# A planner that sets the issue order: urgency from hand-set positions, or from a backward plan

## The chip, the cores and the metric

The kernel runs on one core of a Trainium2 chip. The metric is the device time of that core in microseconds (us), from the chip's own clock. Five engines matter, and each works through its own instructions in the order in which the program has set them down (for TensorE, VectorE and ScalarE the prediction names the page that says so): TensorE (PE; its weight loads are listed as PEld), VectorE (DVE), ScalarE (ACT), GpSimd (POOL) and SyncE (SP), which issues most transfers. A program on one core has no second core to compare with, so beside every time I look at the mean clock that TensorE was granted in that run (1.000 is full speed).

## The reference

It is the forward pass of a speech joint network and all seven gradients, in bf16:

```python
# x [2,16000,256], w1, w2 [3,256,256], g [2,8,256], w_f, w_g, w_o [256,256]
h = gelu(conv3(x, w1))[:, ::2]                       # [2, 8000, 256]
f = gelu(conv3(h, w2))[:, ::2]                       # [2, 4000, 256]
fe, ge = f @ w_f, g @ w_g
j   = tanh(fe[:, :, None, :] + ge[:, None, :, :])    # [2, 4000, 8, 256]
out = j @ w_o
# returns out and the gradients of x, w1, w2, g, w_f, w_g, w_o for a given grad_out [2,4000,8,256]
```

The joint has 8 label positions for each of the 8000 time steps, so `out`, `grad_out` and the products with `w_o` are where most of the bytes and matmuls are.

## The kernel before

The kernel cuts time into 18 chunks over two batches (most of them 512 output steps wide) and does each chunk in stages: A (convolutions, `FE`, and `FER`, which is `FE` transposed), J (joint, `out` and its gradient) and DE (backward to `x`). No stage issues an instruction directly. It *records* operations, with the engines that may run them, a duration by the program's own model, and what they read and write. When everything is recorded, a list scheduler, here called the planner, sets the operations down one by one. The order on each engine, and for many copies the engine itself, come out of this planner (shortened, with comments added; cuts are marked):

```python
class Flow:
    WAKE = {"PE": 45.0, "ACT": 25.0, "DVE": 25.0, "POOL": 280.0, "SP": 60.0}
    MARGIN = 6500.0
    TAIL = {"PE": 180.0, "ACT": 130.0, "DVE": 95.0, "POOL": 40.0, "SP": 0.0}
    # ...
    def op(self, eng, cost, fn, r=(), w=(), new=(), at=None, ..., margin=None):
        o.margin = self.MARGIN if margin is None else margin
        o.prio = (self.now if at is None else at, o.n)      # the hand-set position
        # ... dependences and buffers
    def issue(self):
        # ...
        while left:
            best = None
            for e, lst in avail.items():                    # every engine
                t, cand = T[e], None                        # T: when it is free in the plan
                for o in lst:                               # every operation that is ready
                    s = o.ready + wake                      # ... and its buffers are free
                    k = (max(s, t), o.prio, o, e)
                    if cand is None or k < cand:
                        cand = k
                if cand is not None and (best is None or cand[0] < best[0]):
                    best = cand
            s, _, o, e = best
            T[e] = s + o.cost[o.eng.index(e)]
            if o.work:                                      # a transfer
                # ...
                o.done = ring[e] + 2000.0 + o.margin
            else:
                o.done = T[e] + self.TAIL[e]
            o.inst = o.fn(e)                                # the instruction is emitted here
            # ...
```

Among operations of one engine that could start equally early, the one with the smallest `prio` wins, a position set by hand. And a transfer, unless it is given a margin of its own, is assumed to land 2000 + 6500 ns after its turn on its ring: `MARGIN` is an allowance, so that the plan does not rest on a transfer that comes late.

The copies out of PSUM may go to either of two engines, whichever the planner can start first.

```python
    def evac(dst, src, n, r, w, new=(), scale=None, eng=("ACT", "DVE"), f=1.0):
        # ... a copy by ScalarE or by VectorE
        return op(eng, ..., go, r=r, w=w, new=new)

    # stage A, once per chunk, for mt in 0, 1
    pe_first(mt == 0, "fe", c_pe([W] * KT), mms, r=[(FT, 0), (FT, 1), WF], w=[ps], ...)
    evac(lambda mt=mt: FE[:, mt, :W], lambda ps=ps: ps[:, :W], W, r=[ps], w=[(FE, mt)])
    S["FER"] = to_rows("fer", FE, 0, nb_of[g_] * P, [0, 1, "z"])   # PE transposes FE: 8 matmuls
```

## Time and profile before

| | before |
|---|---|
| time, 3 runs | 800.54 us (800.07 to 802.18) |
| profiled span | 798.8 us |
| TensorE busy / matmul stream worked out | 773.6 us / 762.0 us |
| not stream | 36.8 us |
| VectorE busy, ScalarE busy | 748.7 us, 713.7 us |

"Stream" is what the matmuls alone would take with none ever waiting; the prediction below tells how it is counted. The difference, "not stream", is all that an order can win back, and much of it is fixed (the first input must arrive, the last output must leave). A useful tool is the running sum: at a matmul that both programs have, take its start time and subtract the stream of all matmuls before it. What is left is the time lost up to there. In the trace of before that sum is 20.5 us at 159 us, 23.6 at 429, 25.55 at 567, 28.3 at 765 and 36.8 at the end.

The second is the view of transfers in the last 29 us before the end (what was moved, queue, kind, number, and the median us from issue to landing):

```profile
GHeR<-GHe SPq DMA_TRANSPOSE x2, 3.6
...
HRs<-HTo SPq DMA_TRANSPOSE x2, 2.8
...
NFR<-NGFE SPq DMA_TRANSPOSE x1, 2.4
```

With little other traffic the transposes land 2.4 to 3.6 us after their issue. The planner reckons with 8.5 us plus the transfer itself.

### The profile page before, as it was taken

Reading aid. Unit: us, or ns where it says so; the run is one execution under the profiler, and the core shown is the slowest. Engines: PE = TensorE matmul, PEld = TensorE weight load, DVE = VectorE, ACT = ScalarE, POOL = GpSimd, SP = SyncE. Lnnn points to the kernel's source line nnn. Section 1 sums busy time; section 2 is a strip of 40 time slices with the busy share of each in tenths; the row PEclk is TensorE's granted clock in tenths of the full one; section 3 lists DMA queues with packets and bytes.
Section 4 is the critical chain, followed back from the end, with each engine's and each line's share of the span. In section 5 each row is a group of like instructions: output and inputs, shape, how many; then the busy total and the mean of one; then the engine's idle time right before and its main releaser. Section 6 shows DMA issues by size and latency. Waiting matters only on the chain.

```text
span 798.8 us, 17636 instructions
## 1 busy us (share of the span) xinstructions
PE 773.6 (97%) x6196; PEld 576.0 (72%) x6196; DVE 748.7 (94%) x1752; ACT 713.7 (89%) x1177; POOL 209.1 (26%) x452
## 2 busy tenths in 40 slices
PE   7799999999999999999999999999999999999996
PEld 5566667686776867787877677676776867778885
DVE  4999999998989999998999999998989999999986
ACT  6999999999898989988789999999898989988861
POOL 1212322122222222333232231332222222223242
PEclk9999999999999999999999999999999999999999
DMA  8999999999999999999999999999999998998994
GB/s 205 218 218 226 248 243 228 248 249 273 242 255 245 220 255 192 256 223 256 215 220 209 231 245 240 252 268 257 248 234 246 232 251 208 254 228 206 204 200 104
DMA packets 384701, 184.75 MB, mean 231 GB/s; under 512 B 331716, under 2 KB 368358, under 8 KB 384612
## 3 DMA queue, kind: packets, MB, share of 16 engines
q1 hardware_dynamic: 366644, 133.25, 86.2%
q0 software_dynamic: 15584, 49.19, 18.8%
q10 hardware_dynamic: 2384, 1.18, 0.6%
q8 instruction: 48, 0.79, 0.4%
q14 instruction: 41, 0.34, 0.2%
HBM read 52.48 MB, written 50.34 MB: 129 GB/s over the span
## 4 chain that ended last, share of the span: by engine, by line
PE 66%; DVE 16%; ACT 10%; issue 4%; DMA 2%; POOL 1%; SPq 1%; POOLq 0%; ACTq 0%; DVEq 0%
PE ps L343 56%; PE GWO L343 10%; DVE NGZ L764 3%; DVE ZS L772 2%; DVE g_s L530 2%; ACT JT L697 2%; ACT g_s L536 2%; ACT g_sq L526 1%; ACT OUT_SB L354 1%; ACT FE L354 1%; DMA GOT<-GO_R 1%; DMA XC<-in_x_dram 1%; DVE g_sq L543 1%; PE psb L583 1%; DVE g_sq L541 1%
## 5 line engine op out<-in xcount | busy, mean ns | idle before, releaser
L697 ACT ACTIVATE JT<-FE,GE 128x512 bf16<-128x512 bf16 (+2 forms) x288 | 187.9, 684 | 0.5 <-DVE FE L359 0.2
L371 POOL DMA_DIRECT2D out_dram<-OUT_SB x136 | 94.9, 698 | 347.1 <-ACT OUT_SB L354 285.8
L343 PE MATMUL ps<-GOT,WT 128*128 128x512 bf16 (+3 forms) x640 | 151.9, 332 | 2.1 <-DMA GOT<-GO_R 2.1
L764 DVE SCALAR_TENSOR_TENSOR NGZ<-JSQ,ps 128x512 f32<-128x512 bf16 (+2 forms) x252 | 151.8, 607 | 0.6 <-PE ps L343 0.6
L343 PE MATMUL ps<-WO,JT 128*128 128x256 bf16 x1024 | 151.5, 272 | 0.3 <-DVE g_s L530 0.3
L354 ACT CAST OUT_SB<-ps 128x512 bf16<-128x512 f32 x223 | 132.7, 600 | 15.8 <-PE ps L343 15.7
L717 ACT ACTIVATE JR<-JR 128x1024 bf16<-128x1024 bf16 x128 | 138.1, 1082 | 5.7 <-DVE JR L710 5.4
L343 PE MATMUL GWO<-GO_R,JR 128*128 128x256 bf16 x1024 | 132.7, 273 | 4.3 <-ACT JR L717 4.3
L343 PEld LDWEIGHTS <-JT 128*128 128x128 bf16 x1024 | 98.9, 98 | 46.0 <-issue 1.4
L772 DVE TENSOR_TENSOR ZS<-ZS,NGZ 128x512 f32<-128x512 f32 (+2 forms) x216 | 131.7, 614 | 0.2
L754 ACT ACTIVATE JSQ<-JT 128x1024 bf16<-128x1024 bf16 (+2 forms) x121 | 116.2, 960 | 13.6 <-DVE NGZ L764 12.6
L343 PEld LDWEIGHTS <-JR 128*128 128x128 bf16 x1028 | 99.8, 98 | 26.8 <-ACT JR L717 6.1
L343 PEld LDWEIGHTS <-WT 128*128 128x128 bf16 x1000 | 87.7, 98 | 38.6 <-DMA GOT<-GO_R 2.4
L343 PEld LDWEIGHTS <-W 128*128 128x128 bf16 x792 | 69.7, 98 | 54.4 <-issue 2.8
L343 PE MATMUL ps<-XC,W 128*128 128x512 bf16 (+4 forms) x432 | 92.6, 342 | 2.3 <-DMA XC<-in_x_dram 1.5
L710 DVE TENSOR_TENSOR JR<-FER,GEB 128x1024 bf16<-128x1024 bf16 x128 | 87.5, 685 | 0.4 <-PE GWO L343 0.4
L343 PEld LDWEIGHTS <-X 128*128 128x128 bf16 x768 | 75.0, 98 | 9.6
L530 DVE SCALAR_TENSOR_TENSOR g_s<-g_sq,ps 128x512 bf16<-128x512 bf16 (+2 forms) x108 | 65.9, 612 | 13.4 <-ACT HTo L528 9.2
L343 PE MATMUL ps<-WT,GHo 128*128 128x256 bf16 x384 | 73.3, 273 | 0.5 <-DVE NGZ L764 0.3
L825 DVE TENSOR_TENSOR ACC<-ACC,ps 128x512 f32<-128x512 f32 x96 | 63.8, 679 | 6.0 <-PE ps L343 5.8
L526 ACT ACTIVATE g_sq<-ps 128x512 bf16<-128x512 f32 (+2 forms) x108 | 60.0, 555 | 8.9 <-PE ps L343 8.0
L371 POOL DMA_DIRECT2D out_dram<-GX_SB x70 | 39.1, 559 | 104.3 <-ACT GX_SB L356 49.6
(139 smaller groups left out, 1269.3 us busy)
## 6 DMA issues: line engine op xcount, KB each, us to landing
GO_R<-in_grad_out_dram SPq DMA_DIRECT2D x120, 256.0 KB, 3.9
out_dram<-OUT_SB POOLq DMA_DIRECT2D x120, 256.0 KB, 4.5
X<-in_x_dram SPq DMA_DIRECT2D x28, 576.0 KB, 5.6
out_dram<-GX_SB POOLq DMA_DIRECT2D x60, 256.0 KB, 4.1
GOT<-GO_R SPq DMA_TRANSPOSE x128, 5.3
out_dram<-w_out SPq DMA_DIRECT2D x9, 128.0 KB, 2.0
GO_R<-in_grad_out_dram SPq DMA_DIRECT2D x8, 128.0 KB, 3.2
out_dram<-OUT_SB POOLq DMA_DIRECT2D x8, 128.0 KB, 4.4
```

The costliest lines, as they stand in the source:

```text
L343: nc.tensor.matmul(ps_ap, lhsT=lhsT, rhs=rhs, start=start, stop=stop)
L354: nc.scalar.copy(out=dst(), in_=src())
L371: return eng_.dma_start(out=out(), in_=in_())
L526: op("ACT", c_act(W, True), lambda e, mt=mt, ps=ps: nc.scalar.activation(out=sq[:, mt, :W], in_=ps[:, :W], func=ACT.Square, scale=GELU_SQR ...
L530: op("DVE", c_dve(W), lambda e, mt=mt, ps=ps: nc.vector.scalar_tensor_tensor(out=s[:, mt, :W], in0=sq[:, mt, :W], scalar=1.0, in1=ps[:, :W ...
L697: op("ACT", c_act(W, ptr=True), lambda e, j=j, mt=mt: nc.scalar.activation(out=JT[:, j, mt, :W], in_=S["FE"][:, mt, :W], func=ACT.Tanh, bi ...
L710: op("DVE", c_dve(n * 2 * D, 0.5), lambda e, lo=lo, n=n, m=m, JR=JR: nc.vector.tensor_tensor(out=JR[:m, lo % 2:lo % 2 + n], in0=S["FER"][: ...
L717: op("ACT", c_act(n * 2 * D), lambda e, lo=lo, n=n, m=m, JR=JR: nc.scalar.activation(out=JR[:m, lo % 2:lo % 2 + n], in_=JR[:m, lo % 2:lo % ...
L754: nc.scalar.activation(out=JSQ[:, :, :W], in_=JT[:, j, :, :W], func=ACT.Square)
L764: op("DVE", c_dve(W) + 6, lambda e, d2=d2, ps=ps, u=u, zap=zap, JSQ=JSQ: nc.vector.scalar_tensor_tensor(out=zap(), in0=JSQ[:, d2, :W], sca ...
L772: op("DVE", c_dve(W), lambda e, d2=d2, dst=dst, NGZ=NGZ: nc.vector.tensor_tensor(out=dst[:, d2, :W], in0=ZS[:, d2, :W], in1=NGZ[:, :W], op ...
L825: op("DVE", c_dve(512), lambda e: nc.vector.tensor_tensor(out=acc_ap().rearrange("p k d -> p (k d)"), in0=acc_ap().rearrange("p k d -> p ( ...
```

## The change

The intent: replace the hand-set position by an urgency that follows from the work itself. The planner first runs forward as before. Then it goes backward from the planned end: each operation must be done before the latest start of all that need it, minus the signalling time, and must share its engine with the others that are as late; what comes out is its latest start. That is the new key among operations that could start equally early. Forward and backward are repeated, and the plan is emitted whose TensorE ends first by the planner's own durations. The work is the same: 6196 matmuls before and after. The core of the diff (cut; the rest is bookkeeping so that a plan can be made without being emitted):

```diff
-        o.prio = (self.now if at is None else at, o.n)
+        o.pos = self.now if at is None else at
+        o.key = (o.pos, o.n)
@@
-    def issue(self):
+    def issue(self, passes=3):
+        best = None
+        for k in range(passes + 1):
+            end = self.run(False)
+            if best is None or end < best[0]:
+                best = (end, [o.key for o in self.ops])
+            if k < passes:
+                self.backward(end)
+        for o, key in zip(self.ops, best[1]):
+            o.key = key
+        self.run(True)
+
+    def backward(self, end):
+        # ... succ: for each operation, what needs it, and after what lag
+        for o in sorted(self.ops, key=lambda o: -o.seqn):
+            e, c = o.at[0], o.at[2] - o.at[1]
+            E = end
+            for d, lag in succ[o]:
+                x = late[d] if lag < 0 else late[d] - self.WAKE[d.at[0]] - lag
+                E = min(E, x)
+            # ... move E earlier past what already occupies engine e
+            late[o] = E - c
+        for o in self.ops:
+            o.key = (late[o], o.n)
@@
-                    k = (max(s, t), o.prio, o, e)
+                    k = (max(s, t), o.key, o, e)
```

More of the change, by code (lines that the diff above doesn't have):

```diff
@@ L40 @@
 class Op:
-    __slots__ = ("eng", "cost", "fn", "deps", "succ", "left", "prio", "new", "bufs", "done", "work", "n", "ready", "inst", "hold", "nb", "lead", "margin")
+    __slots__ = ("eng", "cost", "fn", "deps", "succ", "left", "prio", "new", "bufs", "done", "work", "n", "ready", "inst", "hold", "nb", "lead", "margin", "pos", "key", "at", "slotdeps", "seqn")
 class Flow:
@@ L53, in __init__ @@
         self.ctx, self.tc, self.ops, self.slots, self.now, self.seq = ctx, tc, [], {}, 0.0, {}
+        self.bufs = []
     def cls(self, name, n, any_order=False, psum=False):
@@ L57, in cls @@
             name=f"{name}{i}", bufs=1, **({"space": bass.MemoryType.PSUM} if psum else {}))) for i in range(n)]
-        self.slots[name] = [[p, 0.0, None] for p in pools]
+        self.slots[name] = [[p, 0.0, []] for p in pools]
         self.seq[name] = [0, 0, any_order]
@@ L97, in op @@
                 bufs.append(b)
+            self.bufs.append(b)
         o.bufs = bufs
@@ L105, in op, with run @@
         return o
-    def issue(self):
+    def issue(self, passes=3):
[10 more added lines that the diff above has]
+    def backward(self, end):
+        late, busy = {}, {e: [] for e in self.WAKE}
+        succ = {o: [] for o in self.ops}
+        for o in self.ops:
+            for d in o.deps:
+                succ[d].append((o, d.done - d.at[2]))
+            for d in o.slotdeps:
+                succ[d].append((o, self.TAIL[d.at[0]]))
+            for b in o.bufs:
+                if b.born is not None and b.born is not o:
+                    succ[b.born].append((o, -1e9))
+        for o in sorted(self.ops, key=lambda o: -o.seqn):
[4 more added lines that the diff above has]
+                E = min(E, x)
+            iv = busy[e]
+            i = len(iv)
+            while i:
+                lo, hi = iv[i - 1]
+                if hi <= E - c:
+                    break
+                if lo < E:
+                    E = lo
+                i -= 1
+            iv.insert(i, (E - c, E))
+            late[o] = E - c
+        for o in self.ops:
+            o.key = (late[o], o.n)
+    def run(self, emit):
         T = {e: 0.0 for e in self.WAKE}
@@ L112, in issue @@
         left, prog = len(self.ops), -1e12
-        slots, seq = self.slots, self.seq
+        slots = {k: [[p, 0.0, []] for p, _, _ in v] for k, v in self.slots.items()}
+        seq = {k: [v[0], 0, v[2]] for k, v in self.seq.items()}
+        users, use = {}, {}
+        for o in self.ops:
+            o.left = 0
+            for b in o.bufs:
+                users[b] = users.get(b, 0) + 1
+        for o in self.ops:
+            for d in o.succ:
+                d.left += 1
+        num = 0
         def put(o):
@@ L157, in issue @@
             if o.lead:
-                prog = max(prog, o.prio[0])
+                prog = max(prog, o.pos)
             for x in o.eng:
                 avail[x].remove(o)
+            o.slotdeps = []
             for b in o.new:
@@ L164, in issue @@
                 b.slot, slots[b.cls][i][1] = i, None
+                if not seq[b.cls][2]:
+                    o.slotdeps += slots[b.cls][i][2]
+                slots[b.cls][i][2] = []
                 seq[b.cls][1] += 1
-                b.t = slots[b.cls][i][0].tile(b.shape, b.dtype, name=b.name, tag=b.cls)
+                if emit:
+                    b.t = slots[b.cls][i][0].tile(b.shape, b.dtype, name=b.name, tag=b.cls)
             T[e] = s + o.cost[o.eng.index(e)]
@@ L180, in issue @@
                 o.done = T[e] + self.TAIL[e]
-            o.inst = o.fn(e)
-            for h in o.hold:
-                self.tc.add_manual_dep(o.inst.ins, h.inst.ins.name, mybir.DependencyInfo(
-                    mybir.DependencyClass.Sync, mybir.DependencyReason.DATA), reason="order of the first loads")
+            o.at, o.seqn = (e, s, T[e]), num
+            num += 1
+            if emit:
+                o.inst = o.fn(e)
+                for h in o.hold:
+                    self.tc.add_manual_dep(o.inst.ins, h.inst.ins.name, mybir.DependencyInfo(
+                        mybir.DependencyClass.Sync, mybir.DependencyReason.DATA), reason="order of the first loads")
             left -= 1
             for b in o.bufs:
-                b.users -= 1
-                if b.users == 0 and b.cls is not None:
+                if b.cls is not None:
+                    slots[b.cls][b.slot][2].append(o)
+                users[b] -= 1
+                if users[b] == 0 and b.cls is not None:
                     slots[b.cls][b.slot][1] = o.done
@@ L193, in issue @@
                     put(d)
-        self.T = T
+        return T["PE"] if not emit else T
 def c_pe(ns):
```

## The prediction

> **What bounds the kernel now.** I read the profile from coarse to fine: busy times, busy shares in slices, stretches of 20 us, TensorE's waits, and then the timelines of the first 30 us and the last 24 us. The first lines say which engine is fullest and whether that holds all along.
>
> ```profile
> PE 773.6 (97%) x6196; PEld 576.0 (72%) x6196; DVE 748.7 (94%) x1752; ACT 713.7 (89%) x1177; POOL 209.1 (26%) x452
> ...
> PE   7799999999999999999999999999999999999996
> ...
> DVE  4999999998989999998999999998989999999986
> ACT  6999999999898989988789999999898989988861
> ```
>
> TensorE (PE) is busy 97%, but VectorE (DVE, 94%) and ScalarE (ACT, 89%) are close, so I ask stretch by stretch which one is full. The rows below are from the table of 20 us stretches: PE, PEld, DVE, ACT and POOL busy time, then clock, DMA share, GB/s.
>
> ```profile
> 20.00:40.00 20.00, 15.19 (x118) 10.67 (x117) 19.17 (x56) 19.82 (x38) 4.13 (x9) 1.00 1.16 218
> 40.00:60.00 20.00, 18.28 (x136) 12.29 (x136) 19.57 (x53) 19.79 (x33) 3.30 (x7) 1.00 1.04 217
> ...
> 320.00:340.00 20.00, 20.00 (x173) 15.45 (x171) 19.24 (x45) 18.85 (x35) 5.53 (x14) 1.00 1.13 257
> ...
> 780.00:800.00 20.00, 12.38 (x117) 9.83 (x114) 11.18 (x35) 3.36 (x6) 4.76 (x12) 0.92 0.40 102
> ```
>
> Three regimes: from 20 to about 120 us DVE and ACT are both full and PE has holes; from 120 to 760 us PE is full; at the end a chain of dependences runs with every engine partly idle.
>
> A busy PE is not a streaming PE, so I add up the stream itself. Counting matmuls by width (4308 of 256 columns, 1064 of 512, 468 of 128, 168 of 384, 160 of 160 or 32, few others) at columns/2.4 + 2.5 ns, with 25 ns as the least, gives **762.0 us**. The trace supports the rate: in the last run of 256-column weight-gradient matmuls, 22 of them go from 791.60 to 794.01 us, 109.5 ns each against 109.2. So of the 798.8 us span, **36.8 us** is not stream. Doing the same sum per stretch puts 17.2 us of it before 80 us (7.0, 5.4, 2.3, 2.5), 2.2 us at 80 to 120, 7.7 us from 780 us to the end, and the remaining 9.7 us thinly over the 660 us between. TensorE's waits name the holes (total us, times, longest):
>
> ```profile
> PE GWO L343 <- ACT JR L717: 4.3, 5, 1.8
> PE psb L583 <- ACT FE L354: 3.4, 9, 0.5
> PE ps L343 <- DMA GOT<-GO_R: 2.1, 1, 2.1
> PE ps L343 <- DMA XC<-in_x_dram: 1.5, 1, 1.5
> PE ps L343 <- DVE NGFE L772: 1.4, 1, 1.4
> PE ps L343 <- DVE gT L1080: 1.3, 1, 1.3
> ...
> PE psb L583 <- DVE FE L359: 0.7, 2, 0.5
> ```
>
> The second and last rows are the one repeating hole of the middle: once per chunk the transposes of FE come too soon after FE was copied out, 0.3 to 0.5 us, **4.1 us** in all. The others happen at the start or the end.
>
> **What the Trainium skill says.** "TensorE: Matmul & The Clock Gate", section "Back-to-back issue gap", gives columns/2.4 + 2.5 ns for an isolated gap; the trace agrees (above). The same section has about 131 ns for 512 columns in sustained LDWEIGHTS-MATMUL pairs; the trace does not agree: six such matmuls from 18.76 to 20.05 us are 215 ns each, and I use that. "Perfetto Trace Analysis", section "Per-engine timelines", says that ACT and DVE are strict FIFO and that TensorE only pulls weight loads ahead. That is why the program's order matters here: an operation set down too early stalls everything behind it on its engine, as the FE holes show. The same page, section "Optimization Strategy", says a kernel can have several regimes and may gain by interleaving them; the three regimes above are such a case, and a planner's order is what could interleave them.
>
> **The change part by part.** No operation's work is changed: the same 6196 matmuls, the same buffers, the same transfers. Before, the planner ran once, and among operations that could start equally early took the one with the smallest hand-set position. Now it runs forward, then computes backward from the end how late each operation may start, uses that as urgency, repeats three times, and emits the plan whose TensorE ends first by its own durations. Comparing the two programs' orders per engine shows what moved:
>
> 1. *FE gets more lead.* I counted how many ns of matmul stream stand in the program between the copy of FE and its transposes. With ACT as the copier, 39 of 81 uses had under 1000 ns before, 15 of 97 now; the 5% point goes from 551 to 820 ns. The copy takes 584 ns (ACT) plus signalling, so most of the 4.1 us of holes should close: estimate **-3.0 us**. FT (16 uses under 1000 ns, now 6) and GF (12, now 4) move likewise: their waits are small, with the batch switch near 430 us (hole 1.1 us) I put **-1.0 us**.
> 2. *The choice of engine shifts.* 15 OUT_SB copies, 7 net FE copies of several widths and 3 GX copies go from ACT to DVE, 11 squares (JSQ) from DVE to ACT, 4 FER copies from DVE to ACT; shifts of G1S go to POOL, of GFS to DVE. With durations of the trace: DVE +10.2 (15 x 0.683) +4.6 (FE) +2.0 (GX) -7.5 (11 x 0.684) -2.5 (FER) and about -1.3 for the small ones, **+5.5 us** on DVE; ACT **-0.8 us** (-9.0 -4.0 -1.8 +11.9 +3.6 -1.5). In the middle this is free: DVE has 50 us of idle time. In the first 120 us it isn't. When the stream has reached 80 us, the new order has set down about 5 us more of DVE and ACT work together than the old one; those two engines have only 3.4 us of idle time between 20 and 100 us, so about 1.6 us over two engines is real delay: estimate **+1.0 us**.
> 3. *The very start.* The loads of WF and WO now come before W2, and the GEB matmuls before the second convolution. This moves the second convolution later by perhaps 1 to 2 us. But the first product with GOT waits for its transfer in the old trace:
>
> ```profile
> 26.89 1.05 PE L343 MATMUL ps<-GOT,WT 128*128 128x256 bf16 x8 [2.10 <-DMA GOT<-GO_R]
> ```
>
> The work set before that product is the same in both orders, and so are the transfers ahead of it. The 2.1 us absorb the delay: **0**.
>
> 4. *The end.* The old order ran all 24 weight-gradient matmuls of the previous block and then stood 1.43 us at NGFE (row above). The new one puts 8 of them between each pair of NGFE and GF products, which fills that hole: **-1.4 us**. In exchange, the X rows of the last block can be loaded only after those matmuls have freed their buffer, and the load now stands in SP's queue behind the transpose GHeR. In the old trace that transpose was issued at 788.69 us and PE came for X at 791.6, 2.9 us later; now X needs 1.26 (issue of GHeR) + 0.6 (its own) + about 2 (landing, from the 2.0 us of w_out) = 3.9 us: **+1.0 us**. The 4.6 us after the last matmul stay.
>
> Sum: -3.0 -1.0 +1.0 +0 -0.4 = **-3.4 us**; 800.5 - 3.4 = 797.1, which I round to **797.2 us**.
>
> **The rivals.** *A: the start gets clearly shorter.* 17.2 us are lost before 80 us; if the backward plan postpones work that isn't urgent, PE could gain 5 to 8 us there, giving 790 to 793 us. For it: that is where a backward plan should help most. Against it: by 80 us of stream the new order has done more DVE and ACT work, not less. *B: the real machine punishes the plan.* Waits on single DMA arrivals appear because latest-time urgency drops slack that the hand-set positions had; at 10 waits of 1 us, 808 us. For it: the DMA share is over 1 in most stretches, and X's least lead at the end falls from 6.2 to 3.1 us of stream. Against it: the median lead of GOT (21.3 to 22.2 us) and GO_R (39.4 to 39.6 us) is unchanged, since buffers and not urgency decide when they start. *C: nothing moves,* 800 us: the FE holes close but DVE, fuller by 5.5 us, opens others.
>
> **Range and chances.** A gain over 2% needs 16 us out of 36.8, of which 7.3 (first input's arrival) and 4.6 (after the last matmul) are out of reach: 0.03. A loss over 2% needs 16 us of new stalls: 0.02. Between A and B the range is 791.5 to 803.5 us.
>
> **What would show it.** Right: the FE waits of TensorE fall from 4.1 to about 1 us; the NGFE wait vanishes and a wait on X of about 1 us appears near the end; the GOT wait near 27 us shrinks; PE's busy time stays at 20 of 20 us in the middle. Wrong: if PE in 20 to 120 us is fuller by 4 us or more, rival A; if new DMA waits turn up in the middle, rival B; if PE's wait for FE stays, step 1 was mis-sized.

## More of the kernel before

Besides the lines that the prediction shows, two views of the trace before are needed later. The first is the pair of 20 us stretches around the point where the second batch begins to flow in (columns: the stretch, its length, busy time of PE, PEld, DVE, ACT, POOL, then clock, DMA share, GB/s):

```profile
420.00:440.00 20.00, 19.36 (x153) 14.04 (x151) 19.72 (x50) 19.62 (x32) 5.11 (x11) 1.00 1.18 211
440.00:460.00 20.00, 20.00 (x141) 13.27 (x139) 19.86 (x44) 20.00 (x32) 5.29 (x13) 1.00 1.10 238
```

VectorE and ScalarE are full here, as they are in the first 120 us, though TensorE is full too.

## The result, and the profile after

The changed kernel took **802.34 us** (median of 6 runs, 800.52 to 803.2) beside 801.36 us for the kernel before in the same rounds (6 runs, 800.07 to 802.63). The ratio is 1.0009, with a 95% interval of 0.9993 to 1.0026: no difference that the runs can tell. (Ratios here are the mean time of one kernel's fast runs over the mean of the other's fast runs of the same rounds, so not quite the ratio of the medians quoted. All runs in this document were correct.) Both kernels' times mostly follow the granted clock: the changed one had 800.52 us at 0.999 and 803.2 at 0.995, the one before 805.97 at 0.99 in a later round (one run of it, 803.79 at 1.000, doesn't fit). At equal clock the two agree: at 0.997 the changed kernel took 801.93 and 802.74, the one before 801.19 to 802.74 over all rounds. That scatter of a few us is as large as what is sought, so the traces must show where the time went.

The head of the page of after, whose columns are those of the prediction's first fence:

```profile
span 800.2 us, 17623 instructions
...
PE 775.6 (97%) x6196; PEld 576.2 (72%) x6196; DVE 754.2 (94%) x1756; ACT 715.2 (89%) x1164; POOL 223.2 (28%) x461
...
DVE  5999999998989999997989999999999999999995
```

VectorE is busy 5.5 us longer, just what counting the moved copies had said. TensorE does the same matmuls in 2 us more. The span is 1.4 us longer than before.

TensorE's waits in the trace of after (what waited, for what, us in all, times, longest):

```profile
PE GWO L412 <- ACT JR L786: 3.3, 3, 1.5
PE psb L652 <- DVE FE L428: 3.2, 4, 1.6
PE ps L412 <- DVE NGZ L833: 2.3, 3, 0.9
...
PE psb L652 <- ACT FE L423: 0.9, 3, 0.5
...
PE ps L412 <- DMA GOT<-GO_R: 0.4, 1, 0.4
```

The waits that the change was to close add up to as much as before, under another name. Waits for FE were 3.4 us on ScalarE and 0.7 on VectorE, 4.1 together; now they are 0.9 on ScalarE and 3.2 on VectorE, 4.1 together again. ScalarE's nine short holes have become three; VectorE's two have become four, and these are longer. Here is one of the four in the timeline of after from 38 to 45 us (start, busy us, engine, line, what, how many; in brackets the idle time before it and what ended that):

```profile
40.75 0.59 ACT L423 CAST FE<-ps 128x512 bf16<-128x512 f32 x1
...
42.92 0.68 DVE L428 CAST FE<-ps 128x512 bf16<-128x512 f32 x1
...
43.66 0.56 PE L652 MATMUL psb<-ident,FE 128*128 128x128 bf16 x7 [1.58 <-DVE FE L428]
```

The first half of FE was copied by ScalarE from 40.75 us, the second by VectorE, which got to it only at 42.92 us, 2.2 us later. The transposes need both. The matmuls that the second copy waits for had ended by 41.58 us, and the trace shows VectorE without a gap from there to the copy: the lead that the plan gave was spent in VectorE's line. This half was VectorE's in the kernel before, too, with a hole of 0.50 us. And the longer hole took the place of others: the running sums of the two traces are only 0.2 us apart at 50 us (14.1 before, 14.3 after).

The stretches of after answer to those shown of before:

```profile
20.00:40.00 20.00, 15.86 (x123) 10.88 (x121) 19.49 (x55) 20.00 (x39) 5.16 (x10) 1.00 1.16 242
40.00:60.00 20.00, 17.23 (x130) 11.71 (x129) 19.64 (x55) 19.61 (x33) 3.24 (x8) 1.00 0.96 206
...
420.00:440.00 20.00, 19.25 (x155) 13.95 (x154) 20.00 (x46) 19.02 (x30) 5.85 (x11) 1.00 1.16 237
440.00:460.00 20.00, 19.22 (x139) 13.08 (x138) 20.00 (x44) 19.91 (x30) 3.89 (x6) 1.00 1.11 252
...
780.00:800.00 20.00, 14.77 (x139) 11.41 (x136) 11.50 (x31) 4.71 (x10) 5.74 (x14) 0.98 0.44 115
```

In 40 to 60 us TensorE has 1.05 us less than before. Around the batch switch VectorE has no idle time at all, 20.00 of 20 in both stretches, and TensorE falls from 20.00 to 19.22 us in the second. In the last stretch TensorE does more (139 matmul instructions where before had 117), in part only because this span ends 1.4 us later; the running sum below is the fairer measure of the end.

At the very end, the wait for NGFE that the prediction named is gone, and the one product that waits noticeably waits for something else. From the timeline of after:

```profile
782.82 0.30 PE L412 MATMUL ps<-NGFE,WT 128*128 128x160 bf16 x2
...
791.05 0.37 PE L412 MATMUL ps<-JR 8*128 8x256 bf16 x2 [0.93 <-ACT JR L423]
...
793.12 0.41 PE L412 MATMUL ps<-GHoR,X 128*128 128x256 bf16 x2
```

The first and last line carry no bracket: neither NGFE nor X was waited for.

The running sum of time lost puts these together. The figures are what each part adds to it, from one trace of each kernel; the right pair is a cleaner one (experiments 3 and 4), in which both profiles had a clock of 0.999 and the same span of 800.3 us, with the marker in parentheses where it differs. (Its sum is 36.8 because its 14 added warm-up matmuls put 1.5 us more into the stream.)

| part | before | after | difference | clean pair: before, after, difference |
|---|---|---|---|---|
| start, to 160 us | 20.5 | 22.2 | +1.7 | 20.3, 21.0, +0.7 |
| 160 to 430 us (520) | 3.1 | 2.5 | -0.6 | 4.2, 5.9, +1.7 |
| 430 (520) to 570 us | 1.95 | 5.0 | +3.05 | 0.5, 1.5, +1.0 |
| 570 to 765 us (733) | 2.7 | 1.4 | -1.3 | 2.2, 1.3, -0.9 |
| from there to the end | 8.5 | 7.1 | -1.4 | 9.6, 7.1, -2.5 |
| sum | 36.8 | 38.2 | +1.4 | 36.8, 36.8, 0.0 |

So the change does move time. It gains 2.7 us (3.4 in the clean pair) after 570 us, and loses 4.15 us (3.4) before.

### The profile page after: what moved, and what is told of

Read it like the earlier page. It is cut to its first block, busy times and chain, and to the rows that moved or that the text cites. A ratio compares the mean times of both kernels' runs of the same rounds, so it can differ in the third digit from the quotient of the medians.

```text
span 800.2 us, 17623 instructions
## 1 busy us (share of the span) xinstructions
PE 775.6 (97%) x6196; PEld 576.2 (72%) x6196; DVE 754.2 (94%) x1756; ACT 715.2 (89%) x1164; POOL 223.2 (28%) x461
## 4 chain that ended last, share of the span: by engine, by line
PE 68%; DVE 19%; ACT 10%; issue 2%; DMA 1%; DVEq 0%; ACTq 0%
PE ps L412 58%; PE GWO L412 9%; DVE NGZ L833 4%; DVE ZS L841 3%; ACT JT L766 2%; DVE g_s L599 2%; DVE JR L779 2%; ACT JR L786 2%; DVE ACC L894 1%; ACT g_sq L595 1%; ACT JSQ L823 1%; DVE g_sq L610 1%; ACT g_s L605 1%; DVE GHo L954 1%; DMA XC<-in_x_dram 1%
## 5 line engine op out<-in xcount | busy, mean ns | idle before, releaser
L766 ACT ACTIVATE JT<-FE,GE 128x512 bf16<-128x512 bf16 (+2 forms) x288 | 182.0, 676 | 5.8 <-PE ps L412 5.6
L786 ACT ACTIVATE JR<-JR 128x1024 bf16<-128x1024 bf16 x128 | 136.4, 1070 | 6.6 <-DVE JR L779 6.5
L823 ACT ACTIVATE JSQ<-JT 128x1024 bf16<-128x1024 bf16 (+2 forms) x132 | 126.6, 960 | 7.7 <-DVE NGZ L833 5.7
L423 ACT CAST OUT_SB<-ps 128x512 bf16<-128x512 f32 x208 | 119.2, 598 | 8.4 <-PE ps L412 8.2
```

Source lines behind the costliest of these rows:

```text
L423: nc.scalar.copy(out=dst(), in_=src())
L766: op("ACT", c_act(W, ptr=True), lambda e, j=j, mt=mt: nc.scalar.activation(out=JT[:, j, mt, :W], in_=S["FE"][:, mt, :W], func=ACT.Tanh, bi ...
L786: op("ACT", c_act(n * 2 * D), lambda e, lo=lo, n=n, m=m, JR=JR: nc.scalar.activation(out=JR[:m, lo % 2:lo % 2 + n], in_=JR[:m, lo % 2:lo % ...
L823: nc.scalar.activation(out=JSQ[:, :, :W], in_=JT[:, j, :, :W], func=ACT.Square)
```

## The experiments

Fourteen kernels ran. Each time is compared with the kernel before in the same rounds on the same chip. In experiments 1, 2, 5, 6 and 9 to 12 the planner's first pass, which is the plan by hand-set positions, is barred from being emitted; the diffs below leave that line out. The expectations call theories by letters.

### 1 and 2: the end alone, and the body alone

Does the change gain at the end and lose in the body? Then keeping the old plan up to 745 planned us (experiment 1) should beat both kernels, and keeping it after that (experiment 2) should lose. The rival: the two are not separable, or nothing is going on and both are as before. `s0` holds the planned starts of the first pass, which is the plan of before.

```diff
             self.backward(end)
+            for o, t in zip(self.ops, s0):
+                if t < 745e3:          # experiment 2: if t >= 745e3
+                    o.key = (t, o.n)
```

> Old order (planned start of the first forward pass as key) for everything the plan starts before 745 us, backward urgency for the rest. Theory T (the backward plan pays with TensorE holes at the start and at the batch switch, 20.8 us of non-stream before 120 us against 19.4 and 29.7 at 550 us against 25.5, for a shorter end): this order keeps the small holes and gets the better end, so 0.5 to 1.5 us under the kernel before (ratio about 0.9985), cumulative non-stream at the last chunk's NGFE product about 30 us, not 31.5. Rival C (the difference is only the clock at the start): within 0.3 us of before. The planner's own estimate is 2.6 us better than before.

> The reverse: backward urgency before 745 us planned, old order after it. Theory T: the payment without the gain, 2 to 3 us over before (ratio about 1.003), with the batch-switch holes (430 to 550 us) of about 3 to 5 us as in the changed kernel. Rival C: same as before within 0.3 us. Rival D (all differences are noise of the plan, not located): anything between 0 and 2 us with holes elsewhere.

Experiment 1: 801.6 us beside 801.62, ratio 0.9993 (0.9973 to 1.0014). Experiment 2: 807.1 us, ratio **1.0065** (1.0044 to 1.0085). The body under the new urgency, with the old end, is clearly slower; its running sum is 22.95 us by 161 us, 30.1 at 572 and 34.2 at the last NGFE product (before: 20.5, 25.55 and 30.5). Part of this is clock: its runs had 0.992 to 0.994. But at 0.994 it took 806.7 to 808.1 us, where before, in other rounds, took 802.7 to 803.9. Experiment 1 has roughly the body of before, and did not get the end of the changed kernel: TensorE still waits 1.0 us for NGFE, and 0.5 us for X, and from 765 us on its trace loses 8.4 us, where before loses 8.5 and the changed kernel 7.1. So the loss in the body is shown by time; the gain at the end, so far, by the traces of the changed kernel alone.

### 3 and 4: is it the clock at the start?

In the trace of after the first 12 us ran partly at a lower clock. This is where each kernel's first convolution starts, after the run of warm-up matmuls, in the timeline of TensorE; first before:

```profile
7.27 1.25 PE L343 MATMUL ps<-XC,W 128*128 128x256 bf16 x10 [1.45 <-DMA XC<-in_x_dram]
```

and after:

```profile
7.21 2.29 PE L412 MATMUL ps<-XC,W 128*128 128x256 bf16 x10 [2.06 <-DMA XC<-in_x_dram]
```

The same ten matmuls took 2.29 us in place of 1.25, following a hole of 2.06 us in place of 1.45; the granted clock from 6 to 12 us was 0.79, 0.50 and 0.86 in stretches of 2 us. A rival explanation of the whole result is therefore that the start's clock hides a gain. A longer warm-up should close that hole in both kernels, and then after should be ahead:

```diff
-        for _ in range(20):
+        for _ in range(34):
@@
-    op("PE", 20 * 215.0, warm_up, r=[(warm, 0)], w=[wps], new=[wps])
+    op("PE", 34 * 215.0, warm_up, r=[(warm, 0)], w=[wps], new=[wps])
```

> Kernel before with 34 instead of 20 warm-up matmuls, so that TensorE does not pause before the first convolution at 7.2 us. Rival C (a half clock in the first convolution: 2.29 us for ten matmuls in the changed kernel's trace, 1.25 in before's): mean clock 0.999 or more in all runs, spread of the times smaller, time lower by up to 1 us on average. Theory T says nothing against that, but expects the same gap between the two orders with warm clocks.

> Changed kernel with 34 warm-up matmuls. Rival C: equal to e3 within 0.3 us, the whole loss of the change being the cold clock. Theory T: about 1 us slower than e3, with the cumulative non-stream at 550 us some 3 us over that of e3.

Before with the long warm-up took 803.78 us, ratio 1.0026 (1.0003 to 1.0049); after with it 802.69 us, ratio 1.0015 (0.9994 to 1.0037). The longer warm-up starts the first convolution 0.34 us later than before (7.61 us), at full clock in both profiles, but does not cure the scatter of clocks over the runs (0.992 to 0.999 in experiment 3). What counts is the comparison of the two profiles, both at 0.999: the same span, 800.3 us. With equal clocks the change still brings nothing, so this rival fell. The trace of after says the same: by 40 us its running sum is 12.5 us, that of before 12.7, so the slow start had already been taken up by shorter waits. The pair is the clean one of the table above.

### 5 and 6: whose order does it, TensorE's or the others'?

Every operation's key was changed at once. Experiment 5 gives the backward urgency to TensorE's operations alone, experiment 6 to all but TensorE's:

```diff
             self.backward(end)
+            for o, t in zip(self.ops, s0):      # s0: the hand-set keys
+                if o.eng != ("PE",):            # experiment 6: ==
+                    o.key = t
```

> Backward urgency as key for TensorE's operations alone; all other engines keep the old positions. Theory T2 (the harm is the new order on VectorE and ScalarE, the good is TensorE's order at the end): holes up to 560 us as in the kernel before (25 to 26 us of non-stream, not 29.7), end as good as in the changed kernel (24 weight-gradient matmuls around NGFE); 1 to 2.5 us under before, ratio about 0.998. Rival P (TensorE's own new order delays the next chunk's VectorE and ScalarE work at the batch switch): 1 to 3 us over before, the batch-switch holes still 4 us.

> The reverse: backward urgency for VectorE, ScalarE, the transfers and POOL, old positions on TensorE. Theory T2: 2 to 4 us over before (ratio about 1.004), with the end of the kernel before. Rival P: at most 1 us over before, the batch-switch holes as in the kernel before (2 us between 430 and 550 us).

Experiment 5: 799.48 us beside 801.95, ratio **0.9968** (0.9951 to 0.9985). Experiment 6: 806.42 us, ratio **1.006** (1.004 to 1.008). They part on either side of 1, and both intervals are clear of it. The gain of experiment 5 lies at the end: its running sum is 20.8 us by 160 us and 28.1 at 762 (before: 20.5 and 28.3), then 28.6 at the last NGFE product with 8.7 us of stream left, where before has 30.5 with the same 8.7 left. Half of that is given back after it, 1.03 us in one wait on VectorE for `ngb`: the sums end at 35.8 and 36.8. Its FE holes are those of before, 4.2 us in all (a row of its waits):

```profile
PE psb L654 <- ACT FE L425: 3.1, 8, 0.5
...
PE psb L654 <- DVE FE L430: 1.1, 2, 0.6
```

So TensorE's new order is worth some 2 us (at a clock of 0.997, 799.4 to 800.2 us beside 801.95; at 1.000, 798.64 and 798.88 beside 800.59 and 800.64, with a third run of before at 803.79), and did not need the FE holes for it. Experiment 6 loses from the start on: 24.9 us by 163 us, 32.0 at 571, 36.4 at the last NGFE product. Its profiled run is the one with the lowest clock, 0.990; but at 0.996 and 0.997 it took 804.9 to 806.1 us, before 801.95 to 802.72, so the loss is there at equal clock. Its timeline shows one way in which a late engine costs more than its lateness:

```profile
28.16 1.86 PE L414 MATMUL ps<-GOT,WT 128*128 128x256 bf16 x8 [3.07 <-DMA GOT<-GO_R]
```

Before has the same product after a hole of 2.10 us, and then its eight matmuls took 1.05 us. Here the hole is 3.07 us and they took 1.86 us, because the clock had been lowered, as the stretch shows in the column after the five engines:

```profile
28.00:30.00 2.00, 1.84 (x9) 1.28 (x9) 1.22 (x6) 1.32 (x2) 0.00 (x0) 0.50 1.20 326
...
34.00:36.00 2.00, 2.00 (x21) 1.79 (x19) 1.83 (x8) 1.11 (x3) 0.69 (x1) 1.00 1.21 296
```

There are 9 matmul instructions in the first of these stretches against 21 at 34 us; in the trace's record of the clock the half speed lasts from 26.7 to 33.5 us. In this run the hole is paid twice. It is not its length alone that decides this: in experiment 10 a hole of 1.42 us had slow matmuls after it as well, 1.72 us for the same eight:

```profile
26.46 1.72 PE L414 MATMUL ps<-GOT,WT 128*128 128x256 bf16 x8 [1.42 <-DMA GOT<-GO_R]
```

### 7: closing the FE holes directly

If the FE holes cost their 4.1 us, then telling the planner of before that a copy of FE lands 700 ns later than its model says should close them and win about 3 to 4 us. The rival: the planner will push something else into the way.

```diff
-                o.done = T[e] + self.TAIL[e]
+                o.done = T[e] + self.TAIL[e] + o.lag          # o.lag: 0.0 unless set
@@
-            evac(lambda mt=mt: FE[:, mt, :W], lambda ps=ps: ps[:, :W], W, r=[ps], w=[(FE, mt)])
+            evac(lambda mt=mt: FE[:, mt, :W], lambda ps=ps: ps[:, :W], W, r=[ps], w=[(FE, mt)]).lag = 700.0
```

> Kernel before, but the planner is told that a copy of FE takes effect 700 ns later, so that the transposes of FE stand later in TensorE's order. It measures my step 1 by itself. If the holes are an order fault, TensorE's waits for FE fall from 4.1 us to under 1 and the time falls 2.5 to 3.5 us (ratio 0.996 to 0.997). Rival F: the holes only move to other waits because VectorE or ScalarE is the limit there: waits for FE fall, time within 1 us of before.

Measured: 801.15 us beside 801.95, ratio 0.9992 (0.9976 to 1.0008). The rival was right in the total, and the theory in the middle. From the waits:

```profile
PE ps L344 <- DMA GHeR<-GHe: 2.5, 1, 2.5
...
PE psb L584 <- ACT FE L355: 0.5, 1, 0.5
```

The FE waits fell to about 0.6 us, and between 162 and 347 us the running sum stood still at 23.3, where that of before grew from 20.8 (at 161 us) to 23.1: the holes of the middle are real losses. But the start came out 2.8 us worse, with a new wait of 2.5 us for a transfer at 129.6 us, and the batch switch about 2 us worse. The likely reason, which was not tested by itself, is that a 700 ns request moves everything after it, in the stretches where VectorE and ScalarE have no room.

### 8: an honest margin at the end

Why does the planner choose a plan that is worse in the body? Its own reckoning (numbers of the planner, not times) puts the end of TensorE at 789.49, 789.36, 788.24 and 790.26 us for the four plans, so it emits the third and *itself* expects to gain 1.25 us. In that plan the time lost before the end is 4 us more than with hand positions (16.7 against 12.7 us at 736 us of stream), and the last 27 us of stream lose 8.2 in place of 13.4 us. It pays 4 us to save 5 in an end that it takes to be long, since it allows each transpose its 6.5 us of margin there. On the chip those transposes land in 2.4 to 3.6 us in all. If this is right, a margin of 500 ns for the transposes of the last two chunks should make it keep the hand positions:

```diff
-            bytes_=KT * n * P * P * 2, new=[R], transpose=True, nb=nb, at=at)
+            bytes_=KT * n * P * P * 2, new=[R], transpose=True, nb=nb, at=at,
+            margin=500.0 if g_ >= NG - 2 else None)
```

> Changed kernel, but the planner counts the row transposes of the last two chunks with 0.5 us of margin instead of 6.5 us; nothing else. The planner itself then keeps its first forward pass, as none of the backward plans ends earlier. Theory T (the 6.5 us margin made a long imaginary end, for whose shortening the backward plan paid elsewhere): start and middle holes of the kernel before, time 0 to 1 us under before. Rival M (the margin is right, landing late matters): new TensorE waits on the row transposes at the end, 1 us or more over before.

With it the planner's four ends are 780.23, 783.52, 784.38 and 784.19, and it emits the first, the plan by hand-set positions. It took 799.79 us beside 801.95, ratio **0.9971** (0.9955 to 0.9988). The running sum is that of before (20.1 at 159 us, 25.6 at 567, 28.2 at 765) up to the end, where the wait for NGFE shrinks from 1.4 to 0.2 us. The time gained is more than the 0 to 1 us expected, but in part that is scatter: at a clock of 1.000 it took 799.25 to 799.82 us and before 800.59 and 800.64 (a third run 803.79), and the two traces differ by 1.0 us (35.8 and 36.8). So the NGFE hole, the only gain of the changed kernel that I had got right, came from too large an allowance for these transfers and can be had by one argument, with no backward plan at all. That the planner's trade was driven by the margin is shown by its choice; that the margin is also why the body of the chosen plan loses on the chip is not.

### 9, 10, 13 and 14: is it the choice of engine?

In the body, both the order on VectorE and ScalarE changed, and which of the two makes a copy. The theory: the choice of engine is the culprit, as the FE holes suggest. Three of these kernels freeze each copy on the engine that it has in the plan of before (9, 10 and 14), and one (13) leaves the choice free:

```diff
             end = self.run(False)
+            if k == 0:
+                for o in self.ops:
+                    if len(o.eng) > 1:
+                        o.cost = (o.cost[o.eng.index(o.at[0])],)
+                        o.eng = (o.at[0],)
```

Experiment 9 is experiment 6 with engines frozen, experiment 10 the whole change with engines frozen:

> As e6 (backward urgency everywhere but on TensorE), but each operation that may run on either of two engines keeps the engine it had in the kernel before. e6 lost 0.6%. Theory G (the harm is the shift of copies to VectorE, 5.5 us more work on an engine that is full at the start and the batch switch): ratio within 1.001 of before, holes before 160 us as in before (about 20.5 us). Rival O (the order itself is the harm: urgent means late work of the end first): still 1.004 or more.

> The changed kernel's planner (backward urgency on all engines) with the engine choices of the kernel before. Theory G: the start and switch holes shrink to nearly those of before and the end's gain stays: 0.997 to 0.999. Rival O: at or over before, 1.000 to 1.004, with 22 us or more of non-stream by 160 us.

Experiment 9: 805.4 us beside 802.12, ratio 1.0046 (1.0026 to 1.0067): hardly better than experiment 6, again with a hole of over 3 us (3.22) at 27 us and the slow matmuls after it. Against the theory. Experiment 10: 800.01 us, ratio **0.9976** (0.9962 to 0.9991), with 20.6 us lost by 159 us as before: for the theory. But freezing also made the planner emit its second plan in place of its third, so two things had changed. The last two separate them: the second plan with free engines (13), and the third with frozen ones (14).

```diff
-            if best is None or end < best[0]:
+            if k == 1:                  # experiment 13; experiment 14: k == 2, with the freeze above
```

> Changed kernel, but the plan of pass 1 is emitted instead of pass 2, engine choices free. Theory G (engine choice is the harm): as the changed kernel or worse, 1.000 to 1.004 of before, against e10's 0.9976. Rival Q (the pass is what matters): within 0.001 of e10.

> Old engine choices, plan of pass 2 emitted. Theory G: 0.998 to 0.999 of before, 2 us or more under the changed kernel's ratio of 1.0009. Rival Q: as the changed kernel, 1.000 to 1.002.

| ratio to before | second plan | third plan |
|---|---|---|
| engines free | 1.0021 (0.9997 to 1.0044) | 1.0009 (0.9993 to 1.0026), the changed kernel |
| engines as before | 0.9976 (0.9962 to 0.9991) | 1.0043 (1.001 to 1.0076) |

Neither rows nor columns agree, so neither the choice of engine nor the plan's number explains the result by itself. Freezing also changed how good the plans are by the planner's own reckoning: built again with each end printed, it puts TensorE's end at 789.36 and 788.24 us for the free pair and at 787.07 and 789.22 for the frozen one, and the plan that it holds to be the shortest is also the fastest on the chip. Experiment 14 has its own accident, as its timeline shows:

```profile
119.80 1.05 PE L414 MATMUL ps<-GFR,HRe 128*128 128x256 bf16 x8 [3.37 <-DMA GFR<-GF]
120.69 3.47 PE L414 MATMUL GWO<-GO_R,JR 128*128 128x256 bf16 x16
```

TensorE stood 3.37 us waiting for a transfer that the plan held to be early enough, and the 16 matmuls that followed at a lower clock (0.71 and 0.50 in the two stretches of 2 us from 120 us) took 3.47 us, where 16 times 109.5 ns, the rate shown in the prediction, would be 1.75. By an estimate from this one trace, the wait and the slow matmuls cost 5.1 us; without them experiment 14 would lie near 0.998, where the theory had put it. So the theory is not shown, and not refuted either.

What is left is a coarser tendency. Leaving out 3 and 4 with their longer warm-up, seven plans let the backward urgency reorder VectorE and ScalarE over the body (after, experiments 2, 6, 9, 10, 13, 14): their ratios scatter from 0.9976 to 1.0065. Those that keep the old keys there (1, 5, 7, 8 and the two below) all lie between 0.9947 and 0.9993. The two ranges overlap, by experiment 10. Which single reordering does the harm stays open; I saw different holes in different plans.

### 11 and 12: putting the parts that work together

TensorE's urgency from the backward plan (5), and the FE lag (7) only where VectorE and ScalarE have room: in chunks 4 to 6 and from 11 on. Experiment 12 adds the margin of 8.

```diff
+                for o, t in zip(self.ops, s0):
+                    if o.eng != ("PE",):
+                        o.key = t
@@
-            evac(...FE...)
+            evac(...FE...).lag = 700.0 if 4 <= g_ <= 6 or 11 <= g_ else 0.0
```

> e5 (backward urgency for TensorE alone, 0.9968) plus the 700 ns of added lag for the copies of FE, only in the chunks where e7 showed no new holes (4 to 6 and from 11 on). If the FE holes are worth their waiting time in the steady middle (e7: no growth of non-stream from 162 to 304 us against 2.0 us), 2 to 2.5 us under e5, ratio about 0.994. If not, equal to e5.

> e11 plus the short margin of e8 for the row transposes of the last two chunks. The planner's end is then realistic. If the two gains at the end are the same gain (both only fill the hole at the last NGFE product), equal to e11 within 1 us; if they add, 1 to 2 us under e11.

Experiment 11 took **797.71 us** (796.79 to 797.76) beside 802.12, ratio **0.9947** (0.9933 to 0.9961): better than both kernels, though by far less than 2%. Against experiment 5 the gain is less sure: that ran in other rounds, and the intervals of the two ratios touch. Experiment 12 took 798.17 us, ratio 0.9956 (0.9938 to 0.9974): the margin adds nothing to it. The hole at NGFE was closed already, and its trace has a new wait of 1.6 us at 788.9 us for the transpose GHeR, so a short margin has its own price. From the page and the waits of experiment 11:

```profile
span 795.0 us, 17635 instructions
...
PE 773.6 (97%) x6196; PEld 576.4 (73%) x6196; DVE 746.8 (94%) x1751; ACT 714.7 (90%) x1177; POOL 209.3 (26%) x453
```

```profile
PE psb L655 <- ACT FE L426: 0.8, 2, 0.5
...
PE psb L655 <- DVE FE L431: 0.5, 1, 0.5
```

VectorE has 7.4 us less to do than in the changed kernel, and the FE waits are 1.3 us. The running sum is 20.2 us at 160 us, 20.75 at 302 (so half a us in 140), 24.1 at 566 and 26.0 at the last NGFE product. Only the profiled run's clock, 1.000, flatters this trace a little; the six times, within 1 us of each other, don't depend on it.

## Why the prediction was right or wrong

The forecast was a gain of 3.4 us, small but of a definite sign. The measured time lies within its range, but there was no gain. Of its signs, the NGFE wait vanished and the GOT wait shrank; but the FE waits stayed at 4.1 us, no wait on X came, and TensorE fell below 20 of 20 us in the middle (19.22). By its steps:

1. **The FE holes, -3.0 us: failed, and this is the largest error.** They were 4.1 us and still are 4.1 us; in the clean pair they went from 3.4 to 2.5 us, so at best 0.9 us of the 3.0 came. In the steady chunks the step worked: leaving out three places, the holes fell from 3.1 to 0.9 us. At the three places VectorE made the copy, and the holes grew from 1.0 to 3.2 us: at 43 us from 0.50 to 1.58, at 523 to 528 us from 0.26 to 1.36, and at 432 us it stayed (0.26 and 0.25). The step counted how much matmul stream stands between a copy and its use. It took no account of where the copy's *own engine* is at that moment: the matmuls before the two copies at 526 us had ended by 525.42 us, and VectorE, which had no gap, began them at 526.21 and 527.41 us. The lead in the program is only a lead if the copying engine is not behind.

   I had counted the copies' move to VectorE in step 2 and did not bring it back to step 1; but the move explains only half of VectorE's 3.2 us, since the copy at 43 us was VectorE's before, too, and in experiment 10, with the engines of before, TensorE still waits 1.54 us for it. The count of leads was also made for ScalarE's copies alone, and a recount from the two programs doesn't give its figures: of 128 uses ScalarE made 100 before and 80 after, 19 and 6 of them with under 1000 ns of lead (the prediction has 39 of 81 and 15 of 97), VectorE 28 and 48, 13 and 9 of them under.

   **The companion term, -1.0 us for FT, GF and the batch switch, had the wrong sign:** the stretch from 430 to 570 us lost 3.05 us more in place of less (the clean pair, counted from 160 to 570 us, 2.7 us more).

2. **The shift of engines, +1.0 us in the first 120 us: right.** VectorE's +5.5 us came out to the tenth (ScalarE's -0.8 did not, it was +1.5). The start lost 1.7 us, and 0.7 us in the clean pair. Nearly all of the 1.7 us gathered between 50 and 120 us, in short waits most of which were for VectorE, so the kind was right as well. The sentence after it failed: "In the middle this is free". The 50 us of VectorE's idle time are those of the whole span; from 120 to 760 us it has 26 us, and the batch switch, where VectorE has 20.00 of 20, is a second full stretch.

3. **The very start, 0: right.** The wait for GOT shrank from 2.10 to 0.40 us, and by 40 us nothing of the delay was left (12.7 and 12.5 us lost).

4. **The end, -1.4 and +1.0 us: the gain was right, the loss did not come.** The hole at NGFE is gone. The wait for X did not appear (793.12 us, no bracket); another of 0.93 us, for JR, did. The end as a whole gained 1.4 us in the two profiles and 2.5 in the clean pair, where I had put 0.4.

Three readings in the prediction's text are off as well, without weight in its sum. Its losses by stretch count matmuls on a border twice: directly they are 17.8 us before 80 us, 2.7 at 80 to 120 and 8.4 in the middle, not 17.2, 2.2 and 9.7 (the 19.4 us before 120 in the expectation of experiment 1 is 20.5 in the running sum). The FE copies that went to VectorE are 8 net, not 7. And 797.1 was rounded to 797.2.

Put together, by the parts of the running sum: the start was predicted at +1.0 and was +1.7 (clean pair +0.7); the body, step 1, at -4.0 and was +1.15 (+1.8), which is -0.6 + 3.05 - 1.3 (1.7 + 1.0 - 0.9); the end at -0.4 and was -1.4 (-2.5). The sum was predicted at -3.4 and was +1.4 (0.0). The body is over 5 us off, and the end gave back 1 to 2 of them.

Of the rivals, the sentence of rival C was nearest: the time stays, and VectorE, fuller by 5.5 us, opens others. Even its "the FE holes close" was too kind: some of the new holes are the FE holes.

One number could have been had before any run: the planner's own expected gain of 1.25 us, in an end that it overstates. I had read the planner's program for what it orders, and not for what it aims at.

**Shown by times:** TensorE's share of the change gains (experiment 5), the rest of it loses when applied alone (6), and the whole change loses when applied to the body alone (2). **Shown by traces or by the planner's own ends:** the FE holes are real losses in the steady middle (7), and the planner's trade rests on its margin at the end (8). **Only argued:** that VectorE's fullness is what makes the body worse, since freezing the engines did not settle it (9, 10, 13, 14). **Open:** which of the reorderings on VectorE and ScalarE does the harm.

## What to carry to other kernels

A planner optimizes what its model says is expensive: before trusting its urgency, compare its assumed durations and landing times with the trace where it makes its trades, here at the end. A lead counted in one engine's stream is worth little if the engine that has to use the lead is full, so look for the stretches where the helper engines have no idle time, and change the order only of the engine that is the bound there. If a change of order moves the time little, apply it to one engine at a time: here two shares of the change that made -0.3% and +0.6% when applied apart lay behind a zero.

## What the Trainium skill lacked or had wrong

- "TensorE: Matmul & The Clock Gate", section "HAM oscillation — how this bites in real kernels", has the rule "no PE-idle gaps >~3.4µs". Here the length of a hole does not decide it by itself. The clock was at 0.50 by the end of holes of 3.07, 3.22 and 3.37 us or soon after (experiments 6, 9, 14), but also after 2.06 us at the start of the changed kernel and after 1.72 and 1.42 us (experiments 1 and 10), while after 2.10 us in the trace of before, 2.22 in experiment 8 and 2.49 in experiment 7 it stayed at 1.00. The page's halving of the clock agrees, its length of gap doesn't: in "What's actually happening" it ties the half speed to at least one idle window of 3413 ns, which none of these holes spans. The length of that window does show: but for the last one of a run, every stretch at half speed in the sixteen traces lasts 3.41 or 6.83 us. In experiment 10 another hole, of 0.97 us, had ended at 23.99 us; whether thin work around a hole counts as idle was not tested.
- The same page, section "Back-to-back issue gap", has about 131 ns for 512 columns in sustained pairs; 215 ns was measured, as the prediction says.
- No page that I found gives the time from issue to landing of a transpose of this kind; the pages have only a rough fixed time for transfers in general. Here it was 2.4 to 3.6 us in the last 29 us, which is what a planner's allowance should be checked against.
